# Linear attention and a feed-forward layer on one core: v and q in runs of 1 KB, double tiles for the sums of w_out, stores in halves, weights loaded in five parts

## The chip, the cores and the metric

The kernel runs on one core of one Trainium2 chip. The core has five engines with a queue each: TensorE (PE, matmuls, with its weight loads shown as PEld), VectorE (DVE), ScalarE (ACT), GpSimd (POOL) and SyncE (SP, which here only issues DMAs). Each engine works through its instructions in program order; semaphores join them. The metric is the device time of one execution in microseconds (us). Before the change it is 853.97 us, the median of three runs (852.92 to 855.26).

## The reference

```python
q_s = softmax(q, over head_dim);  k_s = softmax(k, over the sequence)   # batch 8, heads 8, seq 576, head_dim 64
kv  = einsum('bhsd,bhse->bhde', k_s, v)
x   = einsum('bhsd,bhde->bhse', q_s, kv)          # then laid out as 4608 tokens x 512
h   = x @ w_in                                     # 512 x 2048
g   = h * (1 / (1 + exp(-1.702 * h)))
out = g @ w_out                                    # 2048 x 512, float32
```

## The kernel before

The 4608 tokens are worked in nine blocks t = 0 to 8 of 512. A block's feed-forward part has eight steps; a step takes a pair p of 128-column chunks of the hidden layer, upwards in even blocks and downwards in odd ones. Each float32 matmul is made of three passes over a high and a low part. Blocks 0 and 1 multiply by w_in plainly (`plain1`, L835). From block 2 on `ffn1` (L880) takes seven half-size products in place of eight, with sums of parts of x (`x_sums`, `x_split`) and of w_in (`sums`, made in block 1). The second layer is plain up to block 2 (`ffn2`, L1092); from block 3 on `ffn2s` (L1015) takes seven products for each group G of two steps, with sums of parts of w_out (`sums2`, made in block 2, one pair a step).

The weights arrive as raw words (`load_w`) and are split in block 0 (`conv`). The split w_in, its sums and w_out's sums are stored to DRAM (`kept`, `kept_t`, `kept_u`) and come back by DMAs that POOL issues (`load_kept`, L408, and `load_u`, L954): `wj` and `wt` are double buffers by the parity of p, `w` a ring of eight.

`sums2` (L463 to L479): DVE makes first sums of w_out's parts into `fine`, half of X[1] (L463), then four differences (L470); ACT casts `fine` into `split`, the other half (L481); DVE leaves the remainder in `fine` (L475); SP stores both (L479). Every step uses the same two tiles, so each waits for the store of the step before.

A group of `ffn2s` gathers its products from PSUM into O[0] and O[1], halves d = 0, 1 of two tiles u: the first of a block as a copy by ACT (`fresh`, L1036), the others as DVE additions (L1041). In the last group a block's tiles are stored by SP (`store`, L1047), 512 KB each; the next block's first copy into O waits for them.

The attention of block t runs beside the steps of block t-1: loads of k, v and q by SP (`load_k` L515, `load_v` L546, `load_q` L566); maxima of k over partitions (`k_max`, DVE L580 to L582 and POOL's reduction L586); the exponentials; kv = k'v on PE (`kv_pairs` L675) and its scaling; q's softmax (`q_soft`, whose last multiply is L711); transposes of q on PE (`q_tr`, L724) and the copy to `qT` (L728); the products with kv (`x_pairs`, L745). v goes into `vt`, a tile with a column of ones beside every head, in runs of 256 bytes; q by tokens into `qt`, in runs of 256 bytes too.

The order of each engine's instructions is not written by hand. `Plan` records operations with the keys that they read and write, a cost and a rank. `due` walks back from PE's order of ranks to the time at which each must be done, with a landing time added for a DMA (and `late`, where given); `forward` then runs the engines by a list schedule, the earliest due first, and what it finds is the program's order.

Of the kernel before, what the change touches and what calls it, by code (L numbers as in the profile page):

```python
# [136 lines left out]
def efficient_attention_then_gelu_ffn(  # L137
# [70 lines left out]
    qt = [sb(f"qt{i}", [P, C, 2, D]) for i in range(NP)]  # L208
# [7 lines left out]
    wj = [[sb(f"wj{i}{jj}", [P, 2, KC, P], F32R) for jj in range(2)] for i in range(2)]  # L216
    wts = {}

    def wt(i):
        if i not in wts:  # L220
            wts[i] = sb(f"wt{i}", [P, 2, 4, 2 * P], F32R, tag=f"wt{i}")
        return wts[i]
# [3 lines left out]
    wts[1] = sb("wt1", [P, 2, 4, 2 * P], F32R, tag="wt1")  # L226
# [127 lines left out]

    def conv(p, kind, rank):

        for jj in range(2):
            ff, T = next_tmp(6)
            K = f"wo{p}{jj}"
            KD = K if kind == "wo" else ("wj", p % 2, jj)  # L360

            def w(jj=jj):
                return words(raws[p, jj])

            def dst(s, jj=jj):
                return wo[p, jj][:, :, s] if kind == "wo" else wj[p % 2][jj][:, s].rearrange("p c f -> p (c f)")

            if kind == "wo":
                fv = ff.rearrange("p (d f) -> p d f", d=2)
            else:  # L370
                fv = ff
# [12 lines left out]
            plan.add("ACT", 0.62, (T,), (KD,), rank, c5)  # L384
            plan.add("DVE", 0.69, (KD, T), (KD,), rank, c6)
            if kind == "wi":

                def run_s(jj=jj):
                    nc.sync.dma_start(
                        out=kept[p][jj], in_=wj[p % 2][jj].bitcast(F32).rearrange("p s c f -> p (s c f)")  # L390
                    )

                plan.add("SP", plan.ISSUE, (KD,), (("kept", p, jj),), rank, run_s, size=2 * DM * P * 4)

# [5 lines left out]
    def load_kept(t, step):  # L400
        if step < 2:
            return
        p = pair(t, step)
        i = p % 2

        def add(off, key, ring, out, src, size):
            plan.add(
                "POOL", 1.0, (key,), (ring,), R(t, step - 2, off), lambda: nc.gpsimd.dma_start(out=out(), in_=src), size=size  # L408
            )

        if t > 1:
            add(4, ("kept_t", p), ("wt", i), lambda: wt(i).rearrange("p s n f -> p (s n f)"), kept_t[p], 4 * DM * 4 * P)
        for jj in range(2):
            out, src = wj[i][jj], kept[p][jj].rearrange("p (s c f) -> p s c f", s=2, c=KC)
            if t > 1 and jj:
                out, src = (x[:, :, KC // 2 : KC] for x in (out, src))
            add(4.1 + 0.1 * jj, ("kept", p, jj), ("wj", i, jj), lambda out=out: out, src, 2 * DM * 4 * P)

    def sums(step):
# [6 lines left out]
        def run_f(jj):  # L426
            x = wj[i][jj].bitcast(F32).rearrange("p s c f -> p s (c f)")
            nc.vector.tensor_tensor(
                out=tt[:, 2 * jj : 2 * jj + 2].rearrange("p n f -> p (n f)"), in0=x[:, 0], in1=x[:, 1], op=ALU.add
            )  # L430

        for jj in range(2):
            plan.add("DVE", dve(DM), (("wj", i, jj),), K[2 * jj : 2 * jj + 2], rank, lambda jj=jj: run_f(jj))
# [6 lines left out]

        def run_l():
            nc.vector.tensor_tensor(out=wt(i)[:, 1], in0=tt, in1=wt(i)[:, 0].bitcast(F32), op=ALU.subtract)

        def run_s():
            nc.sync.dma_start(out=kept_t[p], in_=wt(i).bitcast(F32).rearrange("p s n f -> p (s n f)"))

        T = ("wt", i)
        over = [("tmp", n) for n in range(2, 6)] if i == 0 and step < 2 else []
        plan.add("ACT", act(4 * HT), K, (T, *over), rank, lambda: nc.scalar.copy(wt(i)[:, 0], tt))
        plan.add("DVE", dve(4 * HT), (*K, T), (T,), rank, run_l)  # L450
        plan.add("SP", plan.ISSUE, (T,), (("kept_t", p),), rank, run_s, size=4 * DM * P * 4)

    def sums2(step, rank):

        p = NS - 1 - step
        fine, split = (X[1][:, q, 0:4] for q in (1, 0))
        K, H = ([("X", 1, q, n) for n in range(4)] for q in (1, 0))
# [17 lines left out]
        def run_s():  # L477
            for y, x in enumerate((split, fine)):
                nc.sync.dma_start(out=kept_u[p].rearrange("p (i s f) -> p s i f", i=4, s=2)[:, y], in_=x)  # L479
# [51 lines left out]
    def load_v(b, hp, rank):  # L531
# [11 lines left out]

        def run():
            for h in range(2):
                nc.sync.dma_start(  # L546
                    out=vt[hp][:, h, :, 0:D], in_=v[b, 2 * hp + h, 0:SM, :].rearrange("(p c) d -> p c d", c=CM)
                )

        plan.add("SP", 2 * issue(b), (), (("vt", hp),), rank, run, size=3 * SM * D * 4, late=late(b))  # L550

    def load_q(t, hp, rank):
        runs = [(0, 1, 1), (1, 0, 1)] if hp % 2 else [(0, 0, 2)]
        x, K = early_tile("q", hp) if t == 0 else (None, (("qt", hp),))

        def run():
            for b, s0, p0, p1 in parts(t):
                for o, h, m in runs:
                    src = q[b, 2 * hp + h : 2 * hp + h + m, s0 : s0 + (p1 - p0) * C, :]
                    if t == 0:  # L560
                        nc.sync.dma_start(
                            out=x[p0:p1, o : o + m].rearrange("p h c d -> p h (c d)"),
                            in_=src.rearrange("h (p c) d -> p h (c d)", c=C),
                        )
                    else:
                        nc.sync.dma_start(  # L566
                            out=qt[hp][p0:p1, :, o : o + m], in_=src.rearrange("h (p c) d -> p c h d", c=C)
                        )

        plan.add(  # L570
            "SP", issue(t) * len(parts(t)) * len(runs), (), (K[0],), rank, run, size=(3 if t else 2) * TB * D * 4, late=late(t),
# [120 lines left out]

    def q_soft(t, hp, rank):
        m, M, Q = qm[hp % 2].rearrange("p (c h) -> p c h", c=C), ("qm", hp % 2), ("qt", hp)
        x, K, held = qt[hp], Q, ()
        if t == 0:
            x, (K, *held) = early_tile("q", hp)
            x = x.rearrange("p h c d -> p c h d")
# [8 lines left out]
        def run_s():  # L707
# [3 lines left out]
            nc.vector.tensor_tensor(out=qt[hp], in0=x, in1=bc(m, D), op=ALU.mult)  # L711
# [6 lines left out]
    def q_tr(t, hp, rank):  # L718
        bk = next_bank(t)
        pq = bank[bk]  # L720

        def run():
            for c in range(C):
                nc.tensor.transpose(pq[:, c * P : (c + 1) * P], qt[hp][:, c], ident)  # L724

        PB, Q = ("bank", bk), ("qT", hp % 2)
        plan.add("PE", 0.45, (("qt", hp), "ident"), (PB,), rank, run)
# [99 lines left out]
    def plain1(t, step):  # L827
        i, gi = pair(t, step) % 2, step % 2
        for jj, bk in enumerate((Y, Z)):
            PB, g, G = ("bank", bk), X[jj][:, 0, 0:2], ("X", jj, 0)  # L830

            def run(c, jj=jj, bk=bk):
                w, x = wj[i][jj], xp(t, c)
                for e, (l, r) in enumerate(((0, 0), (0, 1), (1, 0))):
                    nc.tensor.matmul(  # L835
                        bank[bk], w[:, l, c, :], x[:, r], start=c == 0 and e == 0, stop=c == KC - 1 and e == 2
                    )

            for c in range(KC):
                XK = (("place", 4 * t + c), "h"), (("place", 4 * t + c), "l")  # L840
                plan.add(
                    "PE", 0.70, (("wj", i, jj), *XK), (PB,), R(t, step, (0, 1, 4, 6, 8, 10, 12, 14.5)[4 * jj + c]),
# [19 lines left out]
        1: (Y, True, 0, 0), 5: (Z, True, "T", 3), 6: (Y, False, "T", 0), 3: (Z, False, 1, 2),  # L862
        7: (Y, False, "T", 2), 2: (Z, True, 0, 2), 4: (Y, False, "T", 1),
    }

    def ffn1(t, step):
# [4 lines left out]
        def product(n):  # L871
            bk, opens, u, at_ = PROD[n]
            K = ("wt", i) if u == "T" else ("wj", i, u)

            def run():
                x = xo(n)
                for c in range(2):
                    for e, (l, r) in enumerate(((0, 0), (0, 1), (1, 0))):
                        w = wt(i)[:, l, at_, c * P : (c + 1) * P] if u == "T" else wj[i][u][:, l, at_ + c, :]
# [70 lines left out]
    def load_u(n, p, rank, more=()):  # L950
# [7 lines left out]
        plan.add("POOL", 1.0, (("kept_u", p),), (("wb", s), *more), rank, run, size=DM * 4 * P)  # L958
# [7 lines left out]
    def ffn2s(t, G, rank):  # L966
# [65 lines left out]
        def gather(b, u, d, to=None, fresh=False):  # L1032
            old = [("tmp", i) for i in range(2)] if t == TS and fresh and u == 0 else []
# [20 lines left out]
        if end:  # L1054
            gather(1, 0, 0)
        total(4, 2, 3, ALU.add)
# [10 lines left out]
        if end:  # L1067
            gather(0, 1, 0, 1)
            gather(2, 1, 0)
            store(1)  # L1070
# [3 lines left out]
        if end:  # L1074
            store(0)
# [41 lines left out]
    def attend(t):  # L1117
# [5 lines left out]
        for hp in range(NP):  # L1123
# [8 lines left out]
            at(n(1.3 + 0.8 * hp), q_soft, t, hp)  # L1132
# [65 lines left out]
```

## Time and profile before

| | |
|---|---|
| median of three runs | 853.97 us |
| profiled execution | 853.13 us, span 851.4 us, mean granted clock 0.992 |
| PE busy | 822.9 us, 97% |
| PEld busy | 748.5 us, 88% |
| DVE busy | 664.6 us, 78% |
| ACT busy | 577.9 us, 68% |
| POOL busy | 197.9 us, 23% |
| moved by DMA | 204.03 MB, mean 240 GB/s |
| chain that ended last | PE 76%, DMA 14%, DVE 6%, ACT 1% |

The shares are over the whole span, and the program has stages with different limits: block 0 converts weights, block 1 makes w_in's sums, block 2 w_out's sums, blocks 3 to 8 only compute. Where PE pauses, the waits by line name what ended the pause, and the chain follows the last instruction back to what released each step. A DMA's time runs from its issue to its landing.

### The profile page before, as it was taken

What the parts mean: (1) busy time and instruction counts of PE and PEld (TensorE: products, weight loads), DVE (VectorE), ACT (ScalarE), POOL (GpSimd) and SP (SyncE); (2) the same over time, 40 slices, a digit from 0 to 9 for tenths busy, and PEclk for the clock granted to TensorE, in tenths of its full rate; (3) what the DMA queues carried; (4) which work ended last, traced back from release to release, by engine and by line L of the source; (5) the groups of instructions that cost most, each with busy time, mean ns of one, the idle gap of its engine ahead of it and who ended that gap; (6) DMA issues with size and microseconds to landing.
All of it is one profiled execution on the core that took longest, in us unless ns stands there. A gap on an engine that the chain in (4) does not pass through costs nothing.

```text
span 851.4 us, 17134 instructions
## 1 busy us (share of the span) xinstructions
PE 822.9 (97%) x6508; PEld 748.5 (88%) x6508; DVE 664.6 (78%) x1284; ACT 577.9 (68%) x1089; POOL 197.9 (23%) x327
## 2 busy tenths in 40 slices
PE   9899999999999899799999999999999999999997
PEld 4587788878888787799999998999999999999996
DVE  8899997989757679579888987678758975686556
ACT  5698879769648567696868675667477845564442
POOL 1000021120023123224223422322223223322330
PEclk9999999999999999899999999999999999999999
DMA  9999935893597897799589957884799478857983
GB/s 281 279 349 357 266 138 183 256 318 147 171 309 221 249 261 221 236 324 310 133 247 311 312 159 251 222 272 112 228 291 286 112 228 271 261 139 251 278 249 96
DMA packets 156466, 204.03 MB, mean 240 GB/s; under 512 B 79072, under 2 KB 116448, under 8 KB 149984
## 3 DMA queue, kind: packets, MB, share of 16 engines
q0 software_dynamic: 47136, 123.23, 48.8%
q1 hardware_dynamic: 109248, 79.71, 31.6%
q8 instruction: 52, 0.85, 0.4%
q14 instruction: 30, 0.25, 0.1%
HBM read 168.30 MB, written 34.60 MB: 238 GB/s over the span
## 4 chain that ended last, share of the span: by engine, by line
PE 76%; DMA 14%; DVE 6%; ACT 1%; SPq 1%; issue 1%; DVEq 0%; ACTq 0%
PE bank L880 27%; PE bank L1015 25%; PE bank L1092 10%; PE bank L835 8%; DMA out<-O 5%; DMA kept_u<-X 4%; DMA raw<-in_moe_w_out 3%; PE bank L675 2%; PE bank L745 1%; PE bank L724 1%; DVE O L1041 1%; DMA qt<-in_q 1%; PE bank L302 1%; DMA vt<-in_v 1%; SPq L515 1%
## 5 line engine op out<-in xcount | busy, mean ns | idle before, releaser
L880 PE MATMUL bank<-xo,wt 128*128 128x256 f32 x1344 | 195.1, 281 | 8.7 <-DVE X L903 4.2
L880 PEld LDWEIGHTS bank<-xo,wt 128*128 128x128 f32 x1344 | 175.4, 189 | 15.3 <-DVE X L903 6.0
L880 PE MATMUL bank<-xo,wj 128*128 128x256 f32 x1008 | 148.8, 283 | 3.4 <-DVE X L903 2.2
L1015 PE MATMUL bank<-w,gl 128*128 128x256 f32 x1008 | 142.9, 280 | 6.7 <-ACT O L1036 5.8
L1015 PE MATMUL bank<-w,gh 128*128 128x256 f32 x1008 | 143.8, 281 | 0.2
L880 PEld LDWEIGHTS bank<-xo,wj 128*128 128x128 f32 x1008 | 131.3, 190 | 7.3 <-DVE X L903 2.6
L1015 PEld LDWEIGHTS bank<-w,gl 128*128 128x128 f32 x1008 | 128.4, 188 | 8.1 <-ACT O L1036 6.8
L1015 PEld LDWEIGHTS bank<-w,gh 128*128 128x128 f32 x1008 | 129.4, 189 | 0.9 <-DVE gh L997 0.5
L408 POOL DMA_DIRECT2D wj<-kept x96 | 59.0, 615 | 305.6 <-PE bank L880 248.4
L903 DVE TENSOR_TENSOR X<-bank,X 128x256 f32<-128x256 f32 x168 | 70.3, 420 | 70.3 <-PE bank L880 64.6
L954 POOL DMA_DIRECT2D w<-kept_u x152 | 81.4, 536 | 173.0 <-PE bank L1015 144.7
L1092 PE MATMUL bank<-w,gh 128*128 128x512 f32 x384 | 120.7, 395 | 0.3 <-DVE w L379 0.3
L909 ACT ACTIVATE X<-X 128x256 f32<-128x256 f32 x168 | 69.0, 416 | 61.2 <-DVE X L903 60.7
L899 ACT COPY X<-bank 128x256 f32<-128x256 f32 x168 | 61.7, 372 | 70.2 <-PE bank L880 64.6
L835 PE MATMUL bank<-xp,wj 128*128 128x512 f32 x384 | 100.6, 396 | 2.5 <-ACT X L850 2.4
L835 PEld LDWEIGHTS bank<-xp,wj 128*128 128x128 f32 x384 | 71.1, 188 | 21.8 <-ACT X L850 2.8
L1041 DVE TENSOR_TENSOR O<-bank,O 128x512 f32<-128x512 f32 x102 | 70.0, 686 | 16.2 <-PE bank L1015 15.2
L1092 PEld LDWEIGHTS bank<-w,gh 128*128 128x128 f32 x384 | 69.9, 189 | 13.9 <-DVE w L379 0.9
L1092 PE MATMUL bank<-w,gl 128*128 128x512 f32 x192 | 75.9, 395 | 0.0
L997 DVE TENSOR_TENSOR gh<-X,gh 128x512 fp32r<-128x512 f32 x84 | 57.2, 684 | 20.3 <-ACT gh L1001 20.0
L986 DVE TENSOR_TENSOR X<-X 128x512 f32<-128x512 f32 x96 | 65.8, 692 | 5.7 <-ACT X L909 4.2
L586 POOL PARTITION_ALL_REDUCE mx<-mx x32 | 35.0, 1107 | 137.8 <-DVE mx L582 137.6
(118 smaller groups left out, 1157.1 us busy)
## 6 DMA issues: line engine op xcount, KB each, us to landing
wt<-kept_t POOLq DMA_DIRECT2D x42, 1024.0 KB, 8.0
w<-kept_u POOLq DMA_DIRECT2D x152, 256.0 KB, 5.0
wj<-kept POOLq DMA_DIRECT2D x54, 512.0 KB, 5.5
wj<-kept POOLq DMA_DIRECT2D x42, 256.0 KB, 4.7
kt<-in_k SPq DMA_DIRECT2D x32, 256.0 KB, 7.4
raw<-in_moe_w_in SPq DMA_DIRECT2D x16, 512.0 KB, 8.2
raw<-in_moe_w_out SPq DMA_DIRECT2D x16, 512.0 KB, 7.6
kept<-wj SPq DMA_DIRECT2D x16, 512.0 KB, 7.5
```

What stands on the lines that cost most here:

```text
L408: "POOL", 1.0, (key,), (ring,), R(t, step - 2, off), lambda: nc.gpsimd.dma_start(out=out(), in_=src), size=size
L835: nc.tensor.matmul(bank[bk], w[:, l, c, :], x[:, r], start=c == 0 and e == 0, stop=c == KC - 1 and e == 2)
L880: nc.tensor.matmul(ph[bk], w, x[:, r, c, :], start=opens and c == 0 and e == 0, stop=c == 1 and e == 2, skip_group_check=True,)
L899: vec("ACT", act(HT), (("bank", bk),), (A(n),), slot, lambda: nc.scalar.copy(a(n), ph[bk]))
L903: nc.vector.tensor_tensor(out=a(n), in0=ph[bk], in1=a(n), op=ALU.add)
L909: vec("ACT", act(HT), K, (A(n),), slot, lambda: nc.scalar.activation(a(n), x, AF.Gelu_apprx_sigmoid), "gelu")
L954: nc.gpsimd.dma_start(out=wo[s, 0][:, 1].rearrange("p s f -> p (s f)"), in_=kept_u[p][:, c * DM : (c + 1) * DM])
L986: nc.vector.tensor_tensor(out=x[:, :, o], in0=x[:, :, n], in1=x[:, :, m], op=op)
L997: nc.vector.tensor_tensor(out=L[s][:, 1], in0=x[:, :, src], in1=L[s][:, 0].bitcast(F32), op=ALU.subtract)
L1015: nc.tensor.matmul(bv(b)[:, h], L[s][:, l, q, h * P : (h + 1) * P], wx[:, r], start=opens and q == 0 and h == 0 and i == 0, stop=q == 1 an ...
L1041: nc.vector.tensor_tensor(out=half(u, to), in0=bv(b), in1=o, op=ALU.add)
L1092: nc.tensor.matmul(bank[c].rearrange("p (d f) -> p d f", d=2), l, r, start=first_ and e == 0, stop=last and e == 2)
```

## The change

- `sums2`: `fine` lies in X[1] in even steps and in O[1] in odd ones; `split` stays. The store is two operations, `split` behind the cast, `fine` behind the remainder, each with `late=2.0`.
- `store`: O[0]'s first half, O[0]'s second half and O[1] are three stores, each with the keys of its own halves.
- `load_kept`: from block 2 on five DMAs a step (256, 512, 256, 256, 512 KB) in place of three; `wj` is laid out by halves of the model dimension, `wt` by its four sums, with a key for each part, so that a part may be loaded when its own product is done. `sums`, `conv` and the indices of the products follow the layout.
- `load_v`: two heads of v come in runs of 1 KB into `qT`, the place of q's transposes; GpSimd copies them to `vt`.
- `load_q`: q lies by heads, in runs of 1 KB. For t > 0 the last multiply of `q_soft` writes the result by tokens into `kt`, k's place, from which `q_tr` reads.

```diff
     def load_kept(t, step):
...
+            plan.add(
+                "POOL", 0.6, (key,), to, R(t, step - 2, off), lambda: nc.gpsimd.dma_start(out=out(), in_=src), size=size
             )
...
+        part_j(0, 0)
+        part_t(0)
+        part_j(1, 1)
+        part_j(0, 1)
+        part_t(1)
...
     def sums2(step, rank):
 
         p = NS - 1 - step
-        fine, split = (X[1][:, q, 0:4] for q in (1, 0))
-        K, H = ([("X", 1, q, n) for n in range(4)] for q in (1, 0))
+        split, H = X[1][:, 0, 0:4], [("X", 1, 0, n) for n in range(4)]
+        if step % 2:
+            fine, K = O[1].rearrange("p u (d f) -> p (u d) f", d=2), [("O", 1, n // 2, n % 2) for n in range(4)]
+        else:
+            fine, K = X[1][:, 1, 0:4], [("X", 1, 1, n) for n in range(4)]
...
         plan.add("ACT", act(4 * HT), K, H, rank, lambda: nc.scalar.copy(split.bitcast(F32R), fine))
+        plan.add("SP", plan.ISSUE, H, (("kept_u", p, 0),), rank, lambda: run_s(0, split), size=2 * DM * P * 4, late=2.0)
         plan.add("DVE", dve(4 * HT), (*K, *H), K, rank, run_l)
-        plan.add("SP", plan.ISSUE, (*K, *H), (("kept_u", p),), rank, run_s, size=4 * DM * P * 4)
+        plan.add("SP", plan.ISSUE, K, (("kept_u", p, 1),), rank, lambda: run_s(1, fine), size=2 * DM * P * 4, late=2.0)
...
+        s = qT[hp % 2]
+
         def run():
-            for h in range(2):
-                nc.sync.dma_start(
-                    out=vt[hp][:, h, :, 0:D], in_=v[b, 2 * hp + h, 0:SM, :].rearrange("(p c) d -> p c d", c=CM)
-                )
-
-        plan.add("SP", 2 * issue(b), (), (("vt", hp),), rank, run, size=3 * SM * D * 4, late=late(b))
+            nc.sync.dma_start(
+                out=s.rearrange("p (h x) -> p h x", h=2),
+                in_=v[b, 2 * hp : 2 * hp + 2, 0:SM, :].rearrange("h (p c) d -> p h (c d)", c=CM),
+            )
+
+        def run_c():
+            nc.gpsimd.tensor_copy(vt[hp][:, :, :, 0:D], s.rearrange("p (h c d) -> p h c d", h=2, c=CM))
+
+        plan.add("SP", issue(b), (), (("qT", hp % 2),), rank, run, size=2 * SM * D * 4, late=late(b))
+        plan.add("POOL", 1.0, (("qT", hp % 2),), (("vt", hp),), rank, run_c)
...
+    def q_ready(t, hp):
+        x, K = (kt[hp], ("kt", hp)) if t else (qt[hp], ("qt", hp))
+        return x.rearrange("p h c d -> p (h c d)").rearrange("p (c x) -> p c x", c=C), K
...
-            nc.vector.tensor_tensor(out=qt[hp], in0=x, in1=bc(m, D), op=ALU.mult)
+            nc.vector.tensor_tensor(out=qx.rearrange("p c (h d) -> p c h d", h=2), in0=x, in1=bc(m, D), op=ALU.mult)
...
-        def store(u):
+        def store(u, ds):
+            cs = slice(ds[0] * HT, (ds[-1] + 1) * HT)
+
             def run():
-                nc.sync.dma_start(out=ov[:, 2 * u : 2 * u + 2, :], in_=O[u])
-
-            plan.add("SP", 0.4, (("O", u, 0), ("O", u, 1)), (("out", t, u),), 0, run, size=2 * P * DM * 4)
+                nc.sync.dma_start(out=ov[:, 2 * u : 2 * u + 2, cs], in_=O[u][:, :, cs])
+
+            plan.add(
+                "SP", 0.4, [("O", u, d) for d in ds], (("out", t, u, ds),), 0, run, size=len(ds) * P * DM * 4
+            )
...
         if end:
             gather(1, 0, 0)
+            store(0, (0,))
...
-            store(1)
+            store(1, (0, 1))
...
         if end:
-            store(0)
+            store(0, (1,))
...
-            at(n(1.3 + 0.8 * hp), q_soft, t, hp)
+            at(n(2.7 + 0.05 * hp if t else 1.3 + 0.8 * hp), q_soft, t, hp)
```

The schedule moves with it. ACT in block 2, before, around the second cast of `sums2` (X0 holds the activations, X1_75 the sums, L1102 reads block 1's plain results out):

```order
L899 COPY X0_74<-bank4_67 128x256
L1102 COPY O0_80<-bank2_65 128x512
L481 CAST X1_75<-X1_75 128x1024
L899 COPY X0_74<-bank4_67 128x256
L689 ACTIVATE kvn1_73<-bank7_70,r_103 128x64 x4
L909 ACTIVATE X0_74<-X0_74 128x256 x3
L920 CAST gh1_77<-X0_74 128x2x256
```

ACT in the same block after the change, from the second cast of `sums2` (now L506) to the third; L932, L942 and L953 are L899, L909 and L920 of before:

```order
L506 CAST X1_75<-O1_81 128x1024
L942 ACTIVATE X0_74<-bank4_67 128x256
L953 CAST gh0_76<-X0_74 128x2x256
L932 COPY X0_74<-bank5_68 128x256
L1142 COPY O0_80<-bank2_65 128x512
L932 COPY X0_74<-bank4_67 128x256 x2
L942 ACTIVATE X0_74<-X0_74 128x256 x3
L953 CAST gh1_77<-X0_74 128x2x256
L506 CAST X1_75<-X1_75 128x1024
```

The cast reads X1 and O1 in turn; all its results go to X1. Nine rows, one step's work less two instructions, stand from one cast to the next.

POOL before, where block 2 ends and the loads for block 3's first groups stand (`w` is the ring for w_out's sums, ISA is the reduction over partitions):

```order
L954 DMA w_773<-kept_u6_142 128x512
L954 DMA w_1108<-kept_u7_143 128x512
L586 ISA mx0_96<-mx0_96 128x128
L586 ISA mx1_97<-mx1_97 128x128
L954 DMA w_588<-kept_u7_143 128x512
L954 DMA w_1188<-kept_u6_142 128x512
L586 ISA mx2_98<-mx2_98 128x128
L408 DMA wj11_109<-kept51_123 128x2x256
L586 ISA mx3_99<-mx3_99 128x128
```

POOL there after the change (L579 is the new copy of v, L613 the reduction, L987 `load_u`):

```order
L579 COPY vt0_86<-qT0_94 128x8x64
L613 ISA mx2_98<-mx2_98 128x128
L579 COPY vt1_87<-qT1_95 128x8x64
L613 ISA mx3_99<-mx3_99 128x128
L987 DMA w_1105<-kept_u7_143 128x512
L579 COPY vt2_88<-qT0_94 128x8x64
L987 DMA w_1180<-kept_u6_142 128x512
L579 COPY vt3_89<-qT1_95 128x8x64
```

The copies stand among the loads; the last one follows a load of `w`, which waits until a product of PE has read the ring's old contents.

PE before, in the block that prepares block 5: the end of the kv products (L675) and the first transpose of q (L724), with the feed-forward products between:

```order
L675 MATMUL bank7_70<-vt3_89,kt3_85 64x65 x8
L675 MATMUL bank7_70<-vl_105,kl_104 64x65 x2
L1015 MATMUL bank3_66<-w_1238,gl0_78 128x256 x6
L880 MATMUL bank4_67<-xo5_2044,wt0_1546 128x256 x6
L1015 MATMUL bank3_66<-w_1188,gl0_78 128x256 x6
L880 MATMUL bank5_68<-xo6_2058,wj00_106 128x256 x6
L724 MATMUL bank6_69<-ident_71,qt0_90 128x128 x4
L880 MATMUL bank4_67<-xo7_2085,wt0_1546 128x256 x6
```

PE after the change, at the same two (L702 and L757 now; the transpose reads kt0):

```order
L702 MATMUL bank7_70<-vl_105,kl_104 64x65 x2
L702 MATMUL bank7_70<-vt3_89,kt3_85 64x65 x8
L702 MATMUL bank7_70<-vl_105,kl_104 64x65 x2
L913 MATMUL bank5_68<-xo6_2065,wj00_106 128x256 x6
L913 MATMUL bank4_67<-xo7_2091,wt0_1493 128x256 x6
L1048 MATMUL bank0_63<-w_591,gh1_77 128x256 x6
L1048 MATMUL bank3_66<-w_764,gl1_79 128x256 x6
L757 MATMUL bank6_69<-ident_71,kt0_82 128x128 x4
```

In both orders four products of six matmuls stand between the kv products and the first transpose; the transpose now reads k's place, which the multiply fills behind the kv products.

## Rows read from the trace of the kernel before

**Rows 1.** Windows: busy us of each engine (instructions), PE's clock, DMA share, GB/s.

```profile
core 0: us, PE busy (x) PEld busy (x) DVE busy (x) ACT busy (x) POOL busy (x), PEclk, DMA share, GB/s
20.00:40.00 20.00, 17.08 (x157) 11.80 (x155) 16.76 (x38) 12.54 (x24) 1.41 (x2) 1.00 0.96 266
218.00:360.00 142.00, 130.35 (x984) 114.76 (x983) 102.83 (x208) 94.09 (x182) 33.32 (x46) 0.96 0.87 248
...
400.00:800.00 400.00, 393.68 (x3491) 386.46 (x3490) 303.63 (x558) 265.28 (x543) 112.55 (x200) 1.00 0.78 230
500.00:540.00 40.00, 38.24 (x319) 37.87 (x318) 27.48 (x51) 23.80 (x50) 10.44 (x19) 0.96 0.71 216
```

**Rows 2.** Chain that ended last, in order of time: start us, us, what.

```profile
33.20 8.27 DMA raw<-in_moe_w_out
...
238.75 11.02 DMA kept_u<-X
...
339.17 10.77 DMA kept_u<-X
...
435.99 8.52 DMA out<-O
```

**Rows 3.** Waits of the span: us in total, times, longest us.

```profile
DVE X L463 <- DMA kept_u<-X: 11.3, 4, 3.6
...
PE bank L880 <- DVE X L903: 6.4, 6, 2.2
...
PE bank L1015 <- ACT O L1036: 5.8, 5, 1.2
```

**Rows 4.** Timeline of SP's queue in block 2, stores of the sums.

```profile
start us, us, engine line op out<-in xcount [idle before <-releaser]
221.07 1.84 SPq L479 DMA_DIRECT2D kept_u<-X  x2
...
237.99 1.40 SPq L479 DMA_DIRECT2D kept_u<-X  x2
```

**Rows 5.** Durations by line and form: busy us, mean ns, idle before.

```profile
L711 DVE TENSOR_TENSOR qt<-qt,qm 128x512 f32<-128x512 f32 x32 | 22.1, 692 | 1.1
...
L470 DVE TENSOR_TENSOR X<-X 128x256 f32<-128x256 f32 x32 | 13.5, 422 | 0.7
...
L463 DVE TENSOR_TENSOR X<-w 128x512 f32<-128x512 f32 x16 | 10.5, 685 | 11.3 <-DMA kept_u<-X 11.3
...
L475 DVE TENSOR_TENSOR X<-X 128x1024 f32<-128x1024 f32 x8 | 9.7, 1218 | 1.7 <-ACT X L481 1.7
...
L481 ACT CAST X<-X 128x1024 fp32r<-128x1024 f32 x8 | 8.4, 1049 | 4.7 <-DVE X L470 4.6
```

**Rows 6.** Timeline of PE at a block's end, same columns.

```profile
442.55 0.84 PE L880 MATMUL bank<-xo,wt 128*128 128x256 f32 x6
443.23 0.84 PE L1015 MATMUL bank<-w,gh 128*128 128x256 f32 x6
445.23 0.97 PE L1015 MATMUL bank<-w,gl 128*128 128x256 f32 x6 [1.16 <-ACT O L1036]
```

**Rows 7.** DMA issues: times, KB each, median us to landing.

```profile
kept_u<-X SPq DMA_DIRECT2D x16, 512.0 KB, 6.7
...
out<-O SPq DMA_DIRECT2D x12, 512.0 KB, 8.3
out<-O SPq DMA_DIRECT2D x12, 256.0 KB, 4.3
```

**Rows 8.** Timeline of SP's queue near the start.

```profile
16.44 11.12 SPq L546 DMA_DIRECT2D vt<-in_v  x8
```

**Rows 9.** DMA queues: packets, MB, share of 16 engines' time.

```profile
q0 software_dynamic: 47136, 123.23, 48.8%
q1 hardware_dynamic: 109248, 79.71, 31.6%
```

**Rows 10.** One line, the reduction: duration ns min/median/max, first and last start.

```profile
L586 POOL PARTITION_ALL_REDUCE mx<-mx x32: 662/737/4550, 6.0 to 480.6; - x32
```

**Rows 11.** Timeline of POOL in block 2.

```profile
255.08 4.55 POOL L586 PARTITION_ALL_REDUCE mx<-mx  x1 [1.80 <-DVE mx L582]
```

More of the change, by code (lines that the diff above doesn't have):

```diff
@@ L207, in efficient_attention_then_gelu_ffn @@
     vt = [sb(f"vt{i}", [P, 2, CM, W]) for i in range(NP)]
-    qt = [sb(f"qt{i}", [P, C, 2, D]) for i in range(NP)]
+    qt = [sb(f"qt{i}", [P, 2, C, D]) for i in range(NP)]
     qT = [sb(f"qT{i}", [P, TB]) for i in range(2)]
@@ L215, in efficient_attention_then_gelu_ffn @@
     kl, vl = sb("kl", [P, H, D]), sb("vl", [P, H, W])
-    wj = [[sb(f"wj{i}{jj}", [P, 2, KC, P], F32R) for jj in range(2)] for i in range(2)]
+    wj = [[sb(f"wj{i}{jj}", [P, 2, 2, HT], F32R) for jj in range(2)] for i in range(2)]
     wts = {}
@@ L353, in next_tmp, with WJ @@
         return (tmp[i] if i < 2 else wide[:, i - 2]), ("tmp", i)
+    def WJ(i, jj):
+        return [("wj", i, jj, d) for d in range(2)]
     def conv(p, kind, rank):
@@ L383, in conv @@
             plan.add("DVE", 0.69, (K, T), (T,), rank, lambda ff=ff, w=w: narrow(ff, w()))
-            plan.add("ACT", 0.62, (T,), (KD,), rank, c5)
-            plan.add("DVE", 0.69, (KD, T), (KD,), rank, c6)
+            plan.add("ACT", 0.62, (T,), KD, rank, c5)
+            plan.add("DVE", 0.69, (*KD, T), KD, rank, c6)
             if kind == "wi":
@@ L404, in load_kept, with add, part_t, part_j @@
         i = p % 2
-        def add(off, key, ring, out, src, size):
+        def add(off, key, to, out, src):
+            size = 4 * P
+            for n in src.shape[1:]:
+                size *= n
             plan.add(
-                "POOL", 1.0, (key,), (ring,), R(t, step - 2, off), lambda: nc.gpsimd.dma_start(out=out(), in_=src), size=size
+                "POOL", 0.6, (key,), to, R(t, step - 2, off), lambda: nc.gpsimd.dma_start(out=out(), in_=src), size=size
             )
[L411 to L417, printed above, removed]
+        if t == 1:
+            for jj in range(2):
+                w = wj[i][jj].rearrange("p d s f -> p (d s f)")
+                add(4.1 + 0.1 * jj, ("kept", p, jj), WJ(i, jj), lambda w=w: w, kept[p][jj])
+            return
+        def part_t(h):
+            src = kept_t[p][:, 2 * h * DM : (2 * h + 2) * DM]
+            to = [("wt", i, 2 * h + n) for n in range(2)]
+            add(h, ("kept_t", p), to, lambda: wt(i)[:, 2 * h : 2 * h + 2].rearrange("p n s f -> p (n s f)"), src)
+        def part_j(jj, d):
+            w = wj[i][jj][:, d].rearrange("p s f -> p (s f)")
+            add(d, ("kept", p, jj), [("wj", i, jj, d)], lambda: w, kept[p][jj][:, d * DM : (d + 1) * DM])
+        part_j(0, 0)
[3 more added lines that the diff above has]
+        part_t(1)
     def sums(step):
@@ L559, in run @@
                     src = q[b, 2 * hp + h : 2 * hp + h + m, s0 : s0 + (p1 - p0) * C, :]
[L560 to L568, printed above, removed]
+                    nc.sync.dma_start(
+                        out=x[p0:p1, o : o + m].rearrange("p h c d -> p h (c d)"),
+                        in_=src.rearrange("h (p c) d -> p h (c d)", c=C),
+                    )
         plan.add(
-            "SP", issue(t) * len(parts(t)) * len(runs), (), (K[0],), rank, run, size=(3 if t else 2) * TB * D * 4, late=late(t),
+            "SP", issue(t) * len(parts(t)) * len(runs), (), (K[0],), rank, run, size=2 * TB * D * 4, late=late(t),
         )
@@ L835, in run @@
                     nc.tensor.matmul(
-                        bank[bk], w[:, l, c, :], x[:, r], start=c == 0 and e == 0, stop=c == KC - 1 and e == 2
+                        bank[bk], w[:, c // 2, l, c % 2 * P : (c % 2 + 1) * P], x[:, r], start=c == 0 and e == 0, stop=c == KC - 1 and e == 2
                     )
@@ L956, in run @@
             )
-        plan.add("POOL", 1.0, (("kept_u", p),), (("wb", s), *more), rank, run, size=DM * 4 * P)
+        plan.add("POOL", 0.6, [("kept_u", p, y) for y in range(2)], (("wb", s), *more), rank, run, size=DM * 4 * P)
     def first_u(rank):
@@ L1032, in gather @@
         def gather(b, u, d, to=None, fresh=False):
-            old = [("tmp", i) for i in range(2)] if t == TS and fresh and u == 0 else []
+            old = []
+            if t == TS and fresh:
+                old = [("O", 1, i, j) for i in range(2) for j in range(2)] if u else [("tmp", i) for i in range(2)]
             o, K = half(u, d), ("O", u, d)
```

74 lines of the change are left out of this document (39 added, 35 removed).

## The prediction

> **What bounds the kernel now.** I read five views in this order: the windows, the chain of waits, the waits by line, the durations by line, and the timeline of one engine at the places that these point to. The windows come first because they say where TensorE (PE) is not busy. From 400 to 800 us, the blocks 4 to 8, it is busy 393.68 of 400 us [rows 1], so the steady part is bound by the matmuls, which this change leaves alone: no arithmetic of the feed-forward part goes. What can be won is idle time and half clock, and the windows show four places. (a) From 218 to 360 us, block 2 and the start of block 3, PE is busy 130.35 of 142 us, 11.65 idle, and the granted clock averages 0.96, so another 0.04 x 142 = 5.7 us are lost to the lower of the two clock levels: 17.3 together. (b) From 400 to 800 us 6.32 us are idle, and from 500 to 540 the clock is 0.96, 1.6 us: 7.9. (c) From 20 to 40 us 17.08 of 20 are busy: 2.9. (d) The end, after the last matmul.
>
> The chain names the causes. In (a) it runs through the store of the sums of w_out, pieces of 11.02 and 10.77 us; in (b) through the store of an output tile, 8.52 us; in (c) through the load of w_out, 8.27 us [rows 2]. The waits say who passes it on to PE: VectorE's (DVE's) first sums L463 wait 11.3 us for the store of the step before, and PE then waits 6.4 us for DVE's L903 behind them; ScalarE's (ACT's) L1036, the first write of a block into O, makes PE wait 5.8 us at five block ends [rows 3].
>
> Why (a) is slow is a sum. The stores start at 221.07, 237.99 and so on, 17 us a step [rows 4]. One step's ring is two L463 (1.37 us), four L470 (1.69), the cast L481 (1.05), the remainder L475 (1.22), all from [rows 5], the issue (0.76, from 237.99 to where the chain's piece begins at 238.75) and the landing 11.02: 17.1. PE needs less: six matmuls of 256 columns take 0.68 us (442.55 to 443.23 [rows 6]); a step of block 2 has seven such products and 24 matmuls of 512 columns, which I take at twice the time, so 7 x 0.68 + 4 x 2 x 0.68 = 10.2 us, an estimate from that row. The latency of a single buffer sets block 2's pace, not any engine.
>
> **The change part by part.**
>
> Sums of w_out (`sums2`). The remainder's tile `fine` now alternates between X[1] and O[1], and the store is in two, the cast's half issued right behind the cast. L463 no longer meets a landing: its tile was stored two steps ago. `split` stays single, so the landing that is late next is the one before ACT's cast: ring = 1.05 + 0.76 + 6.7, the median landing of one 512 KB half [rows 7], = 8.5 us, and at worst 1.05 + 0.76 + 11.02 = 12.8. The order puts the second to the fourth cast about 0.8 of a step apart, 8.2 us; the later ones over a step. So three casts wait 0.3 us each at the median landing, 4.6 each at the worst. Behind a waiting cast on ACT stand the copies out of PE's two banks, and PE is held by those. I take 1 us each, nearer the median, as one store now goes out alone where two went together, and leave 1 us for half clock that does not go. That is 17.3 - 4 = 13.3 us gained; the bounds are 17.3 and 17.3 - 13.8 = 3.5.
>
> Stores at a block's end (`store`). O[0]'s first half now leaves right behind its own last sum, five products before the block's end, and is 256 KB, which land in 4.3 us where 512 KB take 8.3 [rows 7]. The next block's first L1036 waits for that half only, so PE's 1.16 us of waiting at 445.23 [rows 6] goes; the second half is wanted four products of 0.68 us and what stands between them later, 2.7 us at least, which is more than that wait. I take 7.4 of the 7.9 us of (b), as 0.5 of the idle time is not named by these waits; bounds 4 (the lower half of the waits stays) and 7.9. The last store of all is 256 KB instead of 512: 0.5 us, between 0 and 1.
>
> Weights (`load_kept`): five DMAs a step instead of three, the same bytes, each free to start behind its own product. GpSimd (POOL) issues them far ahead; I count nothing, with the issues hidden beside PE's 10 us steps. The copy and the subtraction in block 1's `sums` come as two of half the size, beside the same steps: nothing.
>
> v and q in runs of 1 KB. At the start SP spent 11.12 us on eight v loads ahead of the w_out load [rows 8]; four loads through q's place stand later, and w_out is issued earlier. I take 1.3 us of (c), the half, since more w_in now goes ahead of it; bounds 0 and 2.9. The packets get larger, and here I weigh a rule. The queues show 31.6% of the DMA engines' time for 79.71 MB on SP's queue, where the short runs are, and 48.8% for 123.23 MB on POOL's [rows 9]: 0.40% a MB on both, so the short runs do not show as a cost, and the sum has nothing for them. The Trainium skill ("DMA: Bandwidth & Descriptors", section Specifications) puts the smallest transfer at line rate at 512 B; by it v and q would free DMA time, but as no engine of the steady part waits for bandwidth, the sum by it would be the same.
>
> GpSimd's copy of v, 28 in all, is new, and before has no such row. The nearest is the other GpSimd operation on SBUF, the reduction over partitions: 0.737 us median, 4.550 the longest [rows 10], at 255.08 [rows 11], where DVE works without a pause. Copies stand in POOL's queue between loads that wait for PE; in block 3's start the last copy stands behind a load that waits for a product some half a step, 5 us, before the kv products that need it. At 0.74 us the issue and the copy fit there and cost nothing. At 4.55 two of a block's copies are bare, 9.1 - 5 = 4.1 us a block and 29 over seven blocks. I take 1.5 us in all, near the median; the other end below is 0, as nothing is removed here. The Trainium skill ("SBUF — State Buffer", section "SBUF: two separate sides") says that GpSimd and a DVE operation with two SBUF inputs lock each other out for the whole of one instruction. The long row agrees in kind, but by the rule a copy would lose one DVE operation, 1.22 us at most (L475), and no 3.8; the sum by it has 0 to 1.5 here.
>
> q's last multiply (L711, 0.692 us [rows 5]) now writes into k's place, so it waits for the kv products, and the transposes wait for it. The order leaves four products between the kv products and the first transpose, 4 x 0.68 = 2.7 us, against 0.69 and one DVE operation ahead, at most 1.22: covered. Where DVE reaches the multiply early it stands there, and L903, which frees PE's banks, stands behind it. Bounds 0 and 1.2 us in each of seven blocks, 8.4; I take 0.35 each, 2.4.
>
> **Sum**, against the profiled run's 853.13 us (span 851.4): 853.13 - 13.3 - 7.4 - 0.5 - 1.3 + 1.5 + 2.4 = 834.5. That run is 0.8 below the median of the three, which is within their spread; I forecast 834.5.
>
> **The rivals.**
> 1. The ring only changes engines. Landings stay at 11 us, as SP's queue holds v, k and q loads between the two halves, and ACT waits where DVE did: 12.8 us against 8.2. For it: both 11 us pieces of the chain. Against it: the median of 6.7. Block 2 then gives 3.5 instead of 13.3: 834.5 + 9.8 = 844.3.
> 2. The copies decide, and it is slower. POOL gives a copy several us while DVE works, kv_pairs stands on PE for it, and the multiply, the transposes and the loads behind the copy follow. Place: the kv products of blocks 1 to 7; price 4.1 us a block, 834.5 - 1.5 + 29 = 862. It decides from (853.1 - 833) / 7 = 2.9 us a block. For it: the 4.55 us row, and DVE is busy 102.83 us of the stretch of 142 [rows 1]. Against it: the median row, and POOL is busy 33.32 us there.
> 3. Every idle us goes and nothing new waits: 853.1 - 17.3 - 7.9 - 2.9 - 1 = 824.
>
> **How the numbers follow.** About 0.3%, 2.6 us, is what a measurement of this kernel can tell from no change. The forecast, 827 to 841 by the terms' middles, has 0.60; rival 1 0.14; rival 3 0.12; rival 2 0.09; the rest, 0.05, is where new waits eat just what is won. Faster: 0.60 + 0.14 + 0.12 = 0.86; the same 0.05; slower 0.09. The range takes in rivals 1 and 3 with their margins and leaves out rival 2: 821 to 848.
>
> **What would show it.** Right: PE idle under 5 us and clock 0.98 or more in the stretch of block 2 to 3; the kept_u stores about 10 to 11 us apart; no wait of L1036 for an output store; L579 under 1 us. Wrong: ACT's cast waiting over 2 us for kept_u; PE's kv products waiting for POOL; DVE's multiply waiting for PE with L903 behind it; copies of several us.

## The result and the profile after

The changed kernel takes 825.04 us, the median of four runs (823.26 to 826.45); the kernel before, run beside it, 853.44 us. The ratio is 0.9723, interval 0.9677 to 0.977. The forecast was 834.5 (821 to 848) and faster at 0.86: direction and range hold, and the time is nearly that of rival 3 (824). The ratios, here and below, are taken from the fast runs alone and are not the quotients of the medians beside them (0.9667 here). The kernel before scatters, from 844.58 to 855.26 us in these four runs, and its medians in the four groups of runs of this document are 853.44, 851.68, 851.46 and 848.31. So the size of the gain is known to a few us only: 28.4 us by the medians and about 24 by the ratio, against 18.6 forecast.

The same stretches of the windows as in [rows 1] come first, from the kernel after:

```profile
core 0: us, PE busy (x) PEld busy (x) DVE busy (x) ACT busy (x) POOL busy (x), PEclk, DMA share, GB/s
20.00:40.00 20.00, 19.46 (x180) 13.88 (x179) 17.53 (x40) 14.30 (x27) 1.42 (x2) 1.00 1.09 347
218.00:360.00 142.00, 140.34 (x1120) 126.83 (x1120) 116.32 (x231) 107.01 (x204) 47.21 (x83) 1.00 0.98 284
400.00:800.00 400.00, 399.96 (x3643) 393.36 (x3642) 316.81 (x589) 277.19 (x558) 149.40 (x279) 1.00 0.86 245
500.00:540.00 40.00, 40.00 (x411) 38.51 (x411) 33.39 (x69) 29.67 (x57) 18.05 (x35) 1.00 1.10 308
```

Idle time of PE falls from 11.65 to 1.66 us in block 2 to 3, from 6.32 to 0.04 in the steady part, from 2.92 to 0.54 near the start, and the clock is 1.00 in all of them. The 5.7 and 1.6 us of half clock are gone with the pauses that stood beside them. Of the four signs of being right, the first holds (1.66 us and 1.00 in block 2 to 3).

Stores of the sums on SP's queue: the first row is both halves of step 0, the next two are the halves of step 1, and the last is the cast's half of step 7 (before: 221.07 and then 17 us a step, [rows 4]). Behind them stand the second to fourth casts of ACT and the one cast that met a landing:

```profile
220.53 1.80 SPq L504 DMA_DIRECT2D kept_u<-X  x2
...
227.29 0.53 SPq L504 DMA_DIRECT2D kept_u<-X  x1
228.55 0.52 SPq L504 DMA_DIRECT2D kept_u<-O  x1
...
302.25 0.52 SPq L504 DMA_DIRECT2D kept_u<-X  x1
```

```profile
226.22 1.04 ACT L506 CAST X<-O 128x1024 fp32r<-128x1024 f32 x1
...
237.40 1.04 ACT L506 CAST X<-X 128x1024 fp32r<-128x1024 f32 x1
...
246.53 1.03 ACT L506 CAST X<-O 128x1024 fp32r<-128x1024 f32 x1
...
277.32 1.05 ACT L506 CAST X<-O 128x1024 fp32r<-128x1024 f32 x1 [0.47 <-DMA kept_u<-X]
```

From the first store to the last it is seven steps in 81.72 us, 11.7 us a step, a little over the 10 to 11 of the second sign. The ring on `split` is there, as forecast, but it costs ACT 0.47 us once, where I had put 3 us of PE. The second to fourth casts stand 11.18 and 9.13 us apart, more than the 8.2 that I had read from the order, so each landing had more time. DVE's first sums, which I had free of any landing, still waited for a store twice, 0.5 and 0.4 us. The third sign holds too: L1071, the old L1036, waited for PE and for no store.

```profile
ACT O L1071 <- PE bank L1048: 5.0, 5, 1.5
```

GpSimd's copy of v and the reduction beside it (before, [rows 10]), from the views of their lines:

```profile
L579 POOL COPY vt<-qT x28: 614/650/1642, 40.2 to 560.0; 128x512 f32<-128x512 f32 x28
```

```profile
L613 POOL PARTITION_ALL_REDUCE mx<-mx x32: 660/731/2682, 6.1 to 546.7; - x32
```

The copy takes 0.65 us in the middle and 1.64 at worst, so the fourth sign holds for the median only; no engine waited for a copy.

The queues (before, [rows 9]):

```profile
DMA packets 119061, 204.06 MB, mean 248 GB/s; under 512 B 18624, under 2 KB 63680, under 8 KB 117952
...
q0 software_dynamic: 53856, 123.23, 52.7%
q1 hardware_dynamic: 65120, 79.71, 30.9%
```

SP's queue moves the same 79.71 MB in 65,120 packets instead of 109,248 and takes 30.9% of a shorter span instead of 31.6%: 254 us of the 16 engines' time instead of 269. POOL's queue, with five loads a step, goes the other way, from 48.8% to 52.7%.

### The profile page after: what moved, and what is told of

It reads as the page before. It is cut to its first block, busy times and chain, and to the rows that moved or that the text cites. A ratio compares the mean times of both kernels' runs of the same rounds, so it can differ in the third digit from the quotient of the medians.

```text
span 822.5 us, 17452 instructions
## 1 busy us (share of the span) xinstructions
PE 812.3 (99%) x6508; PEld 740.4 (90%) x6508; DVE 671.6 (82%) x1292; ACT 587.7 (71%) x1105; POOL 248.8 (30%) x439
## 3 DMA queue, kind: packets, MB, share of 16 engines
q0 software_dynamic: 53856, 123.23, 52.7%
q1 hardware_dynamic: 65120, 79.71, 30.9%
## 4 chain that ended last, share of the span: by engine, by line
PE 92%; DMA 4%; DVE 3%; issue 0%; ACT 0%; SPq 0%; DVEq 0%; ACTq 0%
PE bank L913 33%; PE bank L1048 29%; PE bank L1132 14%; PE bank L868 9%; PE bank L702 2%; PE bank L778 2%; PE bank L757 2%; DMA vl<-in_v 1%; DMA raw<-in_moe_w_out 1%; PE bank L302 1%; DMA out<-O 1%; DMA raw<-in_moe_w_in 1%; DMA qT<-in_v 1%; PE bank L650 0%; PE bank L651 0%; DVE raw L343 0%
## 5 line engine op out<-in xcount | busy, mean ns | idle before, releaser
L913 PE MATMUL bank<-xo,wj 128*128 128x256 f32 x1008 | 146.2, 281 | 0.0
L1048 PE MATMUL bank<-w,gl 128*128 128x256 f32 x1008 | 140.9, 279 | 0.9 <-DVE O L1076 0.9
L1048 PE MATMUL bank<-w,gh 128*128 128x256 f32 x1008 | 141.3, 279 | 0.2
L411 POOL DMA_DIRECT2D wj<-kept x138 | 73.2, 530 | 214.1 <-PE bank L913 141.5
L913 PEld LDWEIGHTS bank<-xo,wj 128*128 128x128 f32 x1008 | 129.0, 188 | 2.1 <-ACT gl L1034 0.8
L1048 PEld LDWEIGHTS bank<-w,gh 128*128 128x128 f32 x1008 | 127.5, 188 | 0.7 <-issue 0.3
L987 POOL DMA_DIRECT2D w<-kept_u x152 | 80.5, 530 | 124.5 <-PE bank L1048 93.5
L932 ACT COPY X<-bank 128x256 f32<-128x256 f32 x168 | 61.6, 371 | 60.0 <-PE bank L913 58.2
L942 ACT ACTIVATE X<-X 128x256 f32<-128x256 f32 x168 | 68.5, 415 | 47.1 <-DVE X L936 46.7
L1132 PEld LDWEIGHTS bank<-w,gh 128*128 128x128 f32 x384 | 69.4, 188 | 14.2 <-DVE w L379 1.4
L411 POOL DMA_DIRECT2D wt<-kept_t x84 | 44.5, 530 | 87.3 <-PE bank L913 73.5
```

The lines of the kernel that those rows point to most:

```text
L411: "POOL", 0.6, (key,), to, R(t, step - 2, off), lambda: nc.gpsimd.dma_start(out=out(), in_=src), size=size
L913: nc.tensor.matmul(ph[bk], w, x[:, r, c, :], start=opens and c == 0 and e == 0, stop=c == 1 and e == 2, skip_group_check=True,)
L932: vec("ACT", act(HT), (("bank", bk),), (A(n),), slot, lambda: nc.scalar.copy(a(n), ph[bk]))
L942: vec("ACT", act(HT), K, (A(n),), slot, lambda: nc.scalar.activation(a(n), x, AF.Gelu_apprx_sigmoid), "gelu")
L987: nc.gpsimd.dma_start(out=wo[s, 0][:, 1].rearrange("p s f -> p (s f)"), in_=kept_u[p][:, c * DM : (c + 1) * DM])
L1048: nc.tensor.matmul(bv(b)[:, h], L[s][:, l, q, h * P : (h + 1) * P], wx[:, r], start=opens and q == 0 and h == 0 and i == 0, stop=q == 1 an ...
```

## The experiments

Two readings were held against each other at first. A: each part removes its own wait, and the terms add. B: the short runs of v and q made the landings late, and the other parts matter little. Each kernel below that leaves out or adds a part is planned anew, so its order differs as a whole; the three `x1` kernels keep the order of the changed kernel, row for row. Each ratio is to the kernel before in the same group of runs; a gain in us by a ratio is that share of 850 us. The changed kernel itself ran in the first group only, so a distance from its 825.04 us is one between groups.

**Parts undone from the changed kernel**

```diff
u1_sums   - fine in X[1] or O[1] by turns, two stores        + fine in X[1], both halves stored behind the remainder
u2_store  - store(0, (0,)) early, store(0, (1,))             + store(0, (0, 1)) at the end
u3_parts  - five weight loads a step                         + 1 MB, 512 KB and 256 KB, keys of the whole tiles
u6_vq     - v through qT and GpSimd, q by heads into kt      + v into vt in 256 B runs, q by tokens, in place
u4_v      - v through qT and GpSimd                          + v into vt in 256 B runs (q stays by heads)
```

u1_sums, expected: 

> The changed kernel with the sums of w_out as before: one tile for the first sums, both halves stored in one operation behind the remainder. Theory A (each part pays for its own wait): the ring of 17 us a step is back, VectorE's first sums wait for the store again, and block 2 to 3 loses 12 to 17 us: 837 to 842. Theory B (the short runs of v and q made every landing slow, and the double tile mattered little): the ring is shorter by the quicker landings, 826 to 830.

Measured 834.51 us (833.06 to 835.07), ratio 0.9819 (0.9773 to 0.9866), 9.5 us above the changed kernel by the medians and 8 by the ratios. It lies between the ranges of A and B: DVE's L486 waits 7.9 us for the store, against 11.3 [rows 3]:

```profile
DVE X L486 <- DMA kept_u<-X: 7.9, 3, 3.7
```

u2_store, expected: 

> The changed kernel with O[0] stored whole, 512 KB, behind the block's last sum. Theory A: the first copy of a block into O waits for that store at five ends, 1.2 us of PE each, with or without half clock behind it: 831 to 833. Theory B: the landing is quicker now, and it stays at 825 to 826.

Measured 824.79 us, ratio 0.9707 (0.9666 to 0.9747): no loss. A fails here. The whole tile lands in 4.5 us, where it took 8.3 [rows 7]; steady windows and landings of this kernel:

```profile
360.00:800.00 440.00, 439.96 (x3973) 433.33 (x3972) 347.49 (x641) 304.94 (x616) 165.58 (x307) 1.00 0.84 241
```

```profile
out<-O SPq DMA_DIRECT2D x12, 512.0 KB, 4.5
```

u3_parts, expected: 

> The changed kernel with three weight loads a step as before (1 MB of sums, 512 KB, 256 KB), each behind the last product that reads any of its tile; the layout stays. Theory A: no product waited for weights before, so 825 to 826. Rival: with the attention's work moved later, the loads of whole tiles come too late and PE waits for them in some steps: 828 to 835.

Measured 826.46 us, ratio 0.9728 (0.9691 to 0.9765): not to be told from the changed kernel.

u6_vq, expected: 

> The changed kernel with v and q as before: v by SP in runs of 256 bytes straight into its tile, q by tokens, the multiply in place, no GpSimd copy. Theory A: only the start's stall comes back, 1 to 2.5 us, and 0 to 2 for copies that are gone: 825 to 828. Theory B: landings of the sums and of the output stores become slow again, stalls return in block 2 to 3 and at block ends: 833 to 845.

Measured 847.65 us, from 840.01 to 856.22 in twelve runs, ratio 0.9966 (0.9925 to 1.0007). Nearly the whole gain is lost although the double tile and the split stores stay. A's range, 825 to 828, falls, and the time lies above B's too. Two places of its profile, on DVE, and behind the second one PE, show how:

```profile
250.48 1.29 DVE L489 TENSOR_TENSOR O<-w 128x512 f32<-128x512 f32 x2 [5.41 <-DMA kept_u<-O]
...
369.56 0.69 DVE L727 TENSOR_REDUCE qm<-qt 128x8 f32<-128x512 f32 x1 [5.85 <-DMA qt<-in_q]
```

```profile
371.63 0.58 PE L1041 MATMUL bank<-w,gh 128*128 128x256 f32 x1 [5.07 <-DVE gh L1023]
```

DVE stands at an instruction whose DMA is late, and the additions that PE needs stand behind it. The landing is another one each time: here a store of the sums, there q. These three rows are from its profiled run, one of its quickest (841.57).

u4_v, expected: 

> The changed kernel with v as before (SP straight into its tile, two loads of 128 KB a pair in runs of 256 bytes, no GpSimd copy), q by heads. Undoing both cost 22.6, of which 10.8 came with the short runs at an unchanged order (v 6.9, q 4.0). If the order and SP's issues count for v as the runs do: 836 to 842. If the rest belongs to q, whose k, v and q loads then stand in another order: 830 to 834.

Measured 841.15 us (835.18 to 846.07), ratio 0.9936 (0.9903 to 0.9969). Most of the loss, 16.1 of 22.6 us by the medians, comes with v alone.

**The runs alone, at an unchanged order**

```diff
x1_vshort (v), x1_qshort (q), x1_short (both)
-                out=s.rearrange("p (h x) -> p h x", h=2),
-                in_=v[b, 2 * hp : 2 * hp + 2, 0:SM, :].rearrange("h (p c) d -> p h (c d)", c=CM),
+                out=s.rearrange("p (c h d) -> p c h d", h=2, c=CM),
+                in_=v[b, 2 * hp : 2 * hp + 2, 0:SM, :].rearrange("h (p c) d -> p c h d", c=CM),
```

x1_short, expected: 

> The changed kernel, every instruction in the same place on its engine and every DMA of the same bytes at the same place in its queue, but from block 1 on v and q arrive in runs of 256 bytes (the tile is laid out by tokens, the GpSimd copy reads it so). Theory B, the short runs themselves: packets under 512 B come back to about 79,000, landings of stores and weights stretch at times, PE idles in block 2 to 3 and at block ends, 838 to 850 with a spread of several us between runs. Rival C, the order and SP's longer queue of issues did it: 825 to 828.

x1_vshort, expected: 

> As the run before with v alone in runs of 256 bytes, q in 1 KB. Theory B: v and q have the same bytes, so half of the loss of both, or all of it where v's loads stand right before or behind a store that somebody waits for: 830 to 842. Rival C: 825 to 827.

x1_qshort, expected: 

> As before with q alone in runs of 256 bytes, v in 1 KB. Theory B: the other half, 830 to 842. Rival C: 825 to 827.

Measured: both 835.85 us (831.26 to 839.25), ratio 0.981 (0.9762 to 0.9859); v alone 831.95, ratio 0.9784 (0.9748 to 0.982); q alone 829.02, ratio 0.9742 (0.9707 to 0.9776). Against the changed kernel that is 10.8 us for both and 6.9 and 4.0 singly by the medians, and about 7, 5 and 2 by the ratios; for q alone no loss at all is possible as well. C falls for both and for v, whose quickest run (828.74) is slower than the slowest of the changed kernel. B's range holds for v, while both and q alone came out below it. Where the time goes is shown by SP's queue, first after the change and then with the short runs; the last row of each is a later load of w_out:

```profile
32.64 0.95 SPq L573 DMA_DIRECT2D qT<-in_v  x2
33.92 0.37 SPq L541 DMA_DIRECT2D kt<-in_k  x1
34.50 0.34 SPq L325 DMA_DIRECT2D raw<-in_moe_w_out  x1
...
68.06 0.55 SPq L325 DMA_DIRECT2D raw<-in_moe_w_out  x1
```

```profile
32.63 3.38 SPq L573 DMA_DIRECT2D qT<-in_v  x2
36.06 3.25 SPq L541 DMA_DIRECT2D kt<-in_k  x1
39.40 0.42 SPq L325 DMA_DIRECT2D raw<-in_moe_w_out  x1
...
73.44 2.27 SPq L325 DMA_DIRECT2D raw<-in_moe_w_out  x1
```

The same two loads of 256 KB hold SP 3.38 us instead of 0.95, the next one, k's with unchanged runs, 3.25 instead of 0.37, and the load of w_out behind them leaves 4.9 us later. The queue does not make this up: the later load of w_out leaves 5.4 us later, and it is the one that ACT then waits for. ACT, then PE, of the kernel with short runs, in block 0:

```profile
81.31 0.68 ACT L334 ACTIVATE wide<-raw 128x512 f32<-128x512 f32 x1 [4.79 <-DMA raw<-in_moe_w_out]
```

```profile
85.13 1.65 PE L876 MATMUL bank<-xp,wj 128*128 128x512 f32 x3 [3.05 <-ACT wj L376]
```

and the windows of this stretch, of the changed kernel and then with short runs: behind the pause the clock falls to 0.91 in the mean, which costs another 0.09 x 40 = 3.6 us.

```profile
60.00:100.00 40.00, 39.24 (x213) 29.87 (x209) 38.01 (x75) 35.13 (x58) 3.83 (x4) 1.00 0.97 297
```

```profile
60.00:100.00 40.00, 35.11 (x168) 26.06 (x167) 33.54 (x69) 29.49 (x49) 1.47 (x2) 0.91 0.94 285
```

The stores of the sums (L504) land no later for it, first after the change and then with the short runs:

```profile
DMA to landing us min/median/max: 3.2/6.5/9.5
```

```profile
DMA to landing us min/median/max: 3.3/6.4/8.8
```

So at an unchanged order the short runs did not stretch these landings, as B has it; they held SP's queue for longer.

**Parts done alone on the kernel before**

```diff
x2_vq_only  before + v and q in 1 KB runs (with the weights' layout; sums, stores and three loads as before)
d1_sums     before + fine by turns, two stores of the sums
d2_store    before + store(0, (0,)), store(0, (1,)), store(1, (0, 1))
d3_both     before + the edits of d1_sums and d2_store
```

x2_vq_only, expected: 

> The kernel before with the runs of 1 KB, the GpSimd copy and the weights' layout, but the sums of w_out, the output stores and three weight loads a step as before. Theory B: the boundaries' waits are gone without a split store and the rest of block 2's ring costs the 9.5 us that undoing it cost the changed kernel: 834 to 837. Theory A (stores and loads need their own parts): 842 to 850.

Measured 831.02 us (829.71 to 832.66), ratio 0.9769 (0.9735 to 0.9802): about 20 us from v and q alone, below both expected ranges. The ring of the sums is still there (DVE waits 5.9 us for it), with stores that land in 5.4 us in the middle, against 6.7 [rows 7]; PE has no idle time in 360 to 800:

```profile
360.00:800.00 440.00, 440.00 (x3963) 432.58 (x3963) 352.51 (x650) 308.25 (x616) 133.41 (x245) 1.00 0.80 243
```

d1_sums, expected: 

> The kernel before with the double tile and the two stores of the sums of w_out alone. By the forecast's own term block 2 to 3 gains 3.5 to 17.3, middle 13.3 of 851: 835 to 842 with the block ends as before. By what the runs so far show (undoing it cost the changed kernel 9.5, and v and q alone already give 20): with the short runs left, landings stay uneven, 843 to 848.

Measured 830.79 us (826.82 to 833.25), ratio 0.9797 (0.9755 to 0.9838), about 17 us by the ratio: below both expected ranges, as much as the upper bound of my term, and against B, as v and q stay short here. Its windows:

```profile
217.00:360.00 143.00, 141.82 (x1136) 128.73 (x1135) 109.42 (x217) 112.14 (x210) 39.88 (x57) 1.00 0.98 282
360.00:800.00 440.00, 439.52 (x3969) 432.30 (x3969) 345.09 (x641) 296.89 (x606) 131.30 (x233) 1.00 0.82 241
```

Its profiled run is its quickest (826.82), and in it the waits at block ends are gone from PE too, although its stores are whole and its v and q short. One profile therefore does not price these waits.

d2_store, expected: 

> The kernel before with the output stores in halves alone. Theory A (a store of 512 KB that lands late is what PE waits for, whatever made it late): the five waits at block ends go, 6 to 8 us with the half clock behind one of them: 843 to 846. Theory D (the waits at block ends need the runs of 1 KB to go): 849 to 852.

Measured 842.34 us (837.56 to 846.18), ratio 0.994 (0.991 to 0.9971): about 5 us by the ratio, and A's mechanism holds on the kernel before. PE idles 0.00 us between 360 and 800, and block 2's ring is as it was:

```profile
217.00:360.00 143.00, 133.73 (x1025) 118.08 (x1025) 104.13 (x209) 97.05 (x187) 35.41 (x49) 0.98 0.88 254
360.00:800.00 440.00, 440.00 (x3979) 433.50 (x3976) 344.14 (x639) 297.22 (x610) 133.36 (x237) 1.00 0.84 244
```

d3_both, expected: 

> The kernel before with both, the sums of w_out and the stores in halves, v and q in short runs. If the terms add as forecast: 830 to 836. If the short runs keep other stalls alive, as the run with v and q undone says: 842 to 850 with a spread of several us.

Measured 827.46 us (825.38 to 832.12), ratio 0.9772 (0.973 to 0.9814): the two edits without v and q give about 19 of the 24 us, and the time lies below both expected ranges. B is not the whole either. The changed kernel, which has v and q in 1 KB and five loads besides, is only 2.4 us quicker by the medians and 4 by the ratios, whose intervals overlap.

Neither reading stands. By the ratios sums alone give 17 us, stores alone 5, v and q alone 20, all together 24. Sums and stores add within the intervals (22 against 19); it is v and q that overlap with them. What the runs show is one kind of loss, an in-order engine standing before a late landing, with two cures: take the landing off the engine's path (double tile, stores in halves), or hold SP's queue for less time, so that what stands behind leaves sooner (longer runs). Either cure alone brings most. The waits are in the rows; that the second cure works through the issue time is shown at the one order of the `x1` kernels and argued for the others. Nothing beat the changed kernel clear of noise.

## Why the prediction was right, and where its size was off

- *What bounds it*: right. PE's idle time falls from 28.5 to 10.2 us, and its busy time from 822.9 to 812.3 as the mean clock goes from 0.992 to 1.000; the matmul work is the same, x6508.
- *Sums of w_out, 13.3 (3.5 to 17.3)*: the mechanism was right and the deduction too large. d1_sums gave about 17 by itself, what it did at block ends included. The mis-sized part is the 4 us left for waiting casts and clock: 0.47 us of ACT's wait was seen, none on PE behind it, and no half clock. The median landing, 6.5 us after against 6.7 before, was the right one of my two bounds; the longest landing was 9.5, not 11. The casts also stood further apart than I had read.
- *Stores in halves, 7.4 (4 to 7.9)*: right as a wait (about 5 us alone on the kernel before), wrong as a necessary part. On the changed kernel the whole store costs nothing, since it lands in 4.5 us.
- *Weights in five parts, 0*: confirmed within the intervals on the changed kernel.
- *Start, 1.3*: the idle time from 20 to 40 us fell by 2.4, but over the first 217 us only from 4.65 to 3.22, 1.4.
- *v and q*: the argument was wrong. From equal DMA time a MB (0.40%) I took it that short runs cost nothing beyond the start; that share does not contain SP's issue time, nor what leaves late behind it. At an unchanged order the short runs cost 6.9 us for v and 4.0 for q by the medians, and the whole edit alone gave about 20 on the kernel before. That the sum still came near is in part luck: those 20 us overlap with the sums of w_out, which I had priced in full, and on top of sums and stores (d3_both) no more than 2 to 4 us were left for v, q and the five loads together, close to my 1.3. The Trainium skill ("DMA: Bandwidth & Descriptors", section Specifications) with its 512 B pointed the right way. On the engines' time the runs bear it out only weakly: at the same order SP's queue takes 32.7% of 836.5 us with the short runs, 274 us, against 254.
- *Copies, 1.5, and the multiply, 2.4*: both too dear. Copies took 0.65 us, and PE waited for none; for the multiply PE waited 0.9 us once. The worst copy, 1.64, is 0.99 above the middle, under the 1.22 us of DVE's longest operation that I had worked out. The Trainium skill ("SBUF — State Buffer", section "SBUF: two separate sides") has GpSimd and a DVE operation with two SBUF inputs lock each other out for one instruction. No run here shows that lock as the cause: the DVE operations beside that copy take 0.69 us at most.
- *What a measurement can tell, 0.3%*: too fine for the kernel before, whose four runs lie 1.2% apart.

The 9.5 us between forecast and result are mostly these surcharges: 4 for casts and clock, 1.5 for copies and 1.5 of the 2.4 for the multiply, together 7. Rival 1 did not come, since the landings kept to their median and the casts had more room; rival 2 did not, since the copies stayed short.

Still open is why the short runs are so much dearer beside the five weight loads: u6_vq takes 847.65 us and d3_both 827.46, and they differ in those loads, the time that the plan counts for each, the tiles' layout and the order planned with them. The rows of u6_vq show late landings of the sums and of q; which of these makes them late was not tried apart.

## What to carry to other kernels

Where an engine in a fixed order waits for a DMA, count how long the queue that issues it is held by the DMAs in front, and not only their bytes: runs of 256 bytes added 20 us to 254 of the DMA engines' time here and delayed what stood behind them on the queue by about 5 us. Before adding up the gains of several edits, ask whether they cure the same wait; each may show its full worth alone and none when taken away last. For a new wait whose trigger has a median and a worst case, the median was the better guess here, and the surcharges for waits that no row showed came out too large.

## What the runs showed of the hardware

- The issue of a DMA on SP took longer with short runs: a v load of 256 KB took 0.376 us in the middle in 1 KB runs and 0.650 in 256-byte runs, and up to 2.85. Two lines, of the changed kernel and of the one with short runs:

```profile
L573 SPq DMA_DIRECT2D qT<-in_v x28: 367/376/1251, 32.6 to 551.0; - x28
```

```profile
L573 SPq DMA_DIRECT2D qT<-in_v x28: 601/650/2852, 32.6 to 564.7; - x28
```

- Times scattered more with the short runs. In the kernels with v and q in 1 KB (four to six executions each) the slowest is 2.0 to 3.2 us above the quickest; with v or q short it is 6.4 to 8.7 us in four to six executions, and 8.6 and 10.9 us in the twelve of d2_store and of u4_v. A single profile of such a kernel is one draw: the profiled run that the forecast summed against took 853.13 us, and 11 of the 55 executions of the kernel before in the four groups took longer.
- In the kernel with short runs a pause of 3.05 us on PE was followed by the lower clock level, 1.2 GHz, from 85 to 91 us (clock 0.50; 0.91 in the mean of the 40 us shown above), and cost 3.6 us more. It does not always follow: in d3_both PE pauses 2.8 us in block 0, and the mean clock of that stretch stays at 1.00.

```profile
PE bank L838 <- ACT X L853: 2.8, 1, 2.8
```

```profile
0.00:217.00 217.00, 211.71 (x1245) 161.44 (x1247) 194.46 (x401) 170.09 (x266) 24.30 (x33) 1.00 0.82 252
```
